# Output projection of the last two batches as seven block products instead of eight, with sums made by adding DMAs

## The chip, the cores and the metric

The kernel runs on one core of one Trainium2 chip. The metric is the device time of one execution in microseconds (us). A core has five engines that run side by side and wait for each other by semaphores: PE (TensorE, matrix products), DVE (VectorE), ACT (ScalarE), POOL (GpSimd) and SP (SyncE, which here only issues DMAs). PEld is PE's weight load, which overlaps its matmuls.

## The reference

Causal attention over 4 batches, 12 heads, 448 positions and head size 64 is followed by a gated feed-forward layer on all 1792 tokens:

```
scores = q @ k.T / sqrt(64), causal mask, softmax;  attn = softmax @ v
x   = attn, as [1792 tokens, 768]
g   = x @ w_gate        # 768 x 1536
val = x @ w_val         # 768 x 1536
h   = g * sigmoid(g) * val
out = h @ w_out         # 1536 x 768, float32
```

## The kernel before

**Layout and precision.** Everything is kept transposed: features lie on the 128 partitions and the 448 tokens of one batch along the free dimension. The 768 model features are 6 blocks of 128, the 1536 hidden features 12 blocks. Each float32 operand is split into a high and a low part (`hi` and `lo`, made by a copy and a subtraction, "a split" below), and one block product is three matmuls of 128x128 by 128x448: high by high, high by low, low by high. `halves` splits a block of activations, `weights` or `fetch_weights` loads a 128x768 tile of weights from a scratch copy in DRAM and splits it into `whl`.

**Batches.** Batches 0 and 1 go through `moe`: gate and value products (tile `M`), activation (`activate`, `finish_h`), output products (tile `MO`). Batches 2 (called A) and 3 (called B) are treated together at the end. `early` computes the first half of A's hidden blocks (`hA[0..5]`) and that half's share of A's output, for all six output blocks m, and stores that share in DRAM (`part`, `keepO`). `operands` and `pair(n)`, n = 0 to 5, compute the rest of A's hidden blocks (`hA[6..11]`) and all of B's (`hB[0..11]`) with a scheme of seven products in place of eight: sums of weight tiles and sums of activations are formed first (tiles `S1` to `S4`, `T1` to `T4`), and each product is accumulated into a sum for more than one result (tiles `Bb`, `Be`). `outputs` then does the output products that remain: for each m the second half of A (6 blocks) and all of B (12 blocks).

**Order.** Nothing of the order is fixed by the loops. Each piece of work is an `op` with the engines that may do it, costs, a due time, buffers and dependencies; `Planner.run` walks all operations once, giving each engine the ready operation that is due first, and the instructions are then issued engine by engine in the order found. Due times are sums of stage lengths (`LEN`), offsets and a table of several hundred numbers (`SHIFT`). Each engine works through its own list in order, so an instruction that waits holds up all behind it. All DMAs but a few stand on SP's list.

**Lines of the profile.** L1150 to L1152 are the three matmuls of gate, value and output products, L1466 to L1468 those of `pair`; L400 is a copy on ACT, L403 on DVE, L406 on POOL; L422 and L425 are a two-operand operation on DVE and on POOL; L1097 loads stored weights; L1230 stores a result; L1272 stores to a scratch tensor in DRAM; L1289 copies a half-done gate product out of PSUM; L1488 and L1492 belong to `pair`'s return of that half; L1606 forms a result of A.

The output products of A's first half are these:

```
for m in range(KD):
    prev, rM = project(A, m, range(HF), lambda x: at(4 * HF + 2 * m + x * 2 / HF), lambda f: A * NW + 2 * NF + 2 * m, hA,
                       lambda f: (hh(A, f), hl(A, f)), (A, "part", m), "M")
```

Of the kernel before, what the change touches and what calls it, by code (L numbers as in the profile page):

```python
# [1715 lines left out]
```

## Time and profile before

| | |
|---|---|
| median of 3 runs | 634.03 us (632.47 to 634.48) |
| profiled execution | 632.45 us, of which 630.7 us span from the first to the last instruction |
| PE busy | 623.1 us (99% of the span) |
| DVE busy | 517.0 us (82%) |
| ACT busy | 416.9 us (66%) |
| POOL busy | 251.3 us (40%) |
| granted TensorE clock | 1.00 in every slice |

Busy time is the time in which at least one instruction of the engine was in progress. Two matmuls that follow each other overlap in the records, so a busy PE need not be issuing at its best rate; the distance between the starts of two matmuls tells that.

### The profile page before, as it was taken

The page shows a single profiled execution, that of the slowest core. Times are in us where ns is not written, and L with a number is a line of the kernel's source. Part 1 is how long each engine was busy: PE and PEld are TensorE (multiplying, and loading weights), DVE is VectorE, ACT ScalarE, POOL GpSimd, SP SyncE. Part 2 cuts the span into 40 slices and gives each one's busy share as a digit, 9 for nine tenths or more (in the row PEclk, how much of TensorE's full clock was granted, in tenths as well). Part 3 has the DMA queues.
Part 4 walks back from the last instruction along what each step waited for, and adds up shares of the span by engine and source line. Part 5 has one row for each costly group of instructions (what it writes and reads, how often), then busy time and mean ns, then how long its engine had stood idle before and what let it go on. Part 6 is the DMA issues. An engine that isn't in the chain of part 4 may idle for free.

```text
span 630.7 us, 11116 instructions
## 1 busy us (share of the span) xinstructions
PE 623.1 (99%) x3590; PEld 561.2 (89%) x3590; DVE 517.0 (82%) x1168; ACT 416.9 (66%) x1001; POOL 251.3 (40%) x301
## 2 busy tenths in 40 slices
PE   8999999999999999999999999999999999999997
PEld 5557999999999999999999998889999999999997
DVE  5998999989998998988998889799988889975210
ACT  6998658958997678577687899775554454561110
POOL 3665543444356455435445453440034324440000
PEclk9999999999999999999999999999999999999999
DMA  8979597888996987576677877886444343236301
GB/s 284 333 245 335 139 384 276 281 318 293 307 362 167 320 267 246 149 249 220 177 224 252 271 239 201 251 283 230 136 121 130 129 131 102 86 109 190 105 18 70
DMA packets 72666, 136.07 MB, mean 216 GB/s; under 512 B 18080, under 2 KB 45472, under 8 KB 72608
## 3 DMA queue, kind: packets, MB, share of 16 engines
q1 hardware_dynamic: 72304, 135.04, 65.5%
q8 instruction: 28, 0.46, 0.3%
q10 hardware_dynamic: 304, 0.33, 0.2%
q14 instruction: 30, 0.25, 0.1%
HBM read 98.34 MB, written 37.00 MB: 215 GB/s over the span
## 4 chain that ended last, share of the span: by engine, by line
PE 83%; DVE 6%; DMA 5%; ACT 4%; issue 1%; POOL 0%; ACTq 0%; SPq 0%; DVEq 0%; POOLq 0%
PE M L1150 10%; PE M L1151 10%; PE M L1152 10%; PE MO L1150 9%; PE MO L1151 9%; PE MO L1152 9%; PE S L618 7%; PE O L1017 5%; DMA wr<-wr 3%; PE T L842 2%; PE O L1062 2%; PE Bb L1467 2%; PE Bb L1466 2%; PE Bb L1468 2%; PE Be L1468 1%
## 5 line engine op out<-in xcount | busy, mean ns | idle before, releaser
L1150 PE MATMUL M<-xh,whl 128*128 128x448 f32 x360 | 133.7, 371 | 0.9 <-ACT s L1289 0.7
L1152 PE MATMUL M<-xh,whl 128*128 128x448 f32 x360 | 130.4, 362 | 0.0
L1151 PE MATMUL M<-xl,whl 128*128 128x448 f32 x360 | 130.4, 362 | 0.0
L422 DVE TENSOR_TENSOR whl<-wraw,whl 128x768 fp32r<-128x768 f32 x86 | 83.9, 983 | 21.1 <-ACT whl L400 20.7
L681 ACT ACTIVATE p<-p,m 128x192 f32<-128x192 f32 (+3 forms) x180 | 91.1, 509 | 2.3 <-DVE m L669 2.0
L400 ACT ACTIVATE whl<-wraw 128x768 fp32r<-128x768 f32 x72 | 60.2, 840 | 34.1 <-PE MO L1152 19.8
L1150 PEld LDWEIGHTS M<-xh,whl 128*128 128x128 f32 x360 | 67.5, 188 | 7.8 <-ACT s L1289 2.8
L1152 PEld LDWEIGHTS M<-xh,whl 128*128 128x128 f32 x360 | 67.5, 187 | 4.7
L669 DVE CUSTOM_DVE_ANT_0 p<-S,masks 128x192 f32<-128x192 f32 (+3 forms) x180 | 68.3, 424 | 3.5 <-PE S L618 3.3
L1151 PEld LDWEIGHTS M<-xl,whl 128*128 128x128 f32 x360 | 67.6, 188 | 3.8
L1150 PE MATMUL MO<-h,whl 128*128 128x448 f32 x162 | 59.7, 369 | 0.0
L1151 PE MATMUL MO<-h,whl 128*128 128x448 f32 x162 | 58.7, 362 | 0.0
L1152 PE MATMUL MO<-h,whl 128*128 128x448 f32 x162 | 58.5, 361 | 0.0
L735 ACT ACTIVATE p<-p,rec 128x192 f32<-128x192 f32 (+3 forms) x128 | 53.9, 478 | 4.6 <-DVE rec L692 4.5
L1136 DVE SCALAR_TENSOR_TENSOR wraw<-wide,top 128x768 uint32<-128x768 uint32 x36 | 36.0, 1000 | 1.9 <-ACT top L400 1.8
L900 DVE STREAM_TRANSPOSE w<-p 128x256 f32<-128x256 f32 (+2 forms) x120 | 36.3, 354 | 0.6 <-ACT p L735 0.3
L618 PEld LDWEIGHTS S<-KS,QS 64*128 64x128 f32 (+1 forms) x432 | 29.6, 174 | 6.3 <-issue 4.1
L681 ACT ACTIVATION_READ_ACCUMULATOR p<-p,m 128x1 f32 (+1 forms) x180 | 34.1, 190 | 0.0
L425 POOL TENSOR_TENSOR whl<-wraw,whl 128x768 fp32r<-128x768 f32 x16 | 29.5, 1848 | 9.2 <-DVE whl L422 3.1
L1150 PE MATMUL MO<-last,whl 128*128 128x448 f32 x90 | 33.1, 368 | 0.0
L1151 PE MATMUL MO<-last,whl 128*128 128x448 f32 x90 | 32.6, 363 | 0.0
L1152 PE MATMUL MO<-last,whl 128*128 128x448 f32 x90 | 32.6, 362 | 0.0
(386 smaller groups left out, 1527.5 us busy)
## 6 DMA issues: line engine op xcount, KB each, us to landing
wide<-in_w_dram SPq DMA_DIRECT2D x36, 768.0 KB, 6.8
wraw<-wr SPq DMA_DIRECT2D x66, 384.0 KB, 4.1
wr<-wraw SPq DMA_DIRECT2D x36, 384.0 KB, 4.2
wr<-wr SPq DMA_DIRECT2D x24, 384.0 KB, 3.8
x<-dO SPq DMA_DIRECT2D x12, 608.0 KB, 6.0
vraw<-in_v_dram SPq DMA_DIRECT2D x24, 256.0 KB, 4.4
qraw<-in_q_dram SPq DMA_DIRECT2D x23, 224.0 KB, 5.0
kraw<-in_k_dram SPq DMA_DIRECT2D x23, 224.0 KB, 5.0
```

Of the source, the lines that this page charges most:

```text
L400: nc.scalar.activation(out(), in_(), AF.Copy, scale=scale)
L422: r["DVE"] = (cost("DVE", "two", n), lambda: nc.vector.tensor_tensor(out(), a(), b(), alu))
L618: nc.tensor.matmul(st[u + y][f"S{i}"][:r], Q[:, q0 : q0 + r], K[:, :q1_] if y else K[:, S - q1_ :], start=z == 0, stop=z == len(passes) - 1)
L669: nc.vector.tensor_tensor_reduce(p[:r], s[f"S{i}"][:r], mask[:r, maskX - q0 : maskX - q0 + q1_] if h % 2 else back[:r, P - min(q1_, P) : P ...
L681: nc.scalar.activation(p[:r], p[:r], AF.Exp, bias=peak(i)[:r], scale=-1.0, accum_out=sums[u % NR][:r, i : i + 1],)
L735: nc.scalar.activation(p[:r], p[:r], AF.Copy, scale=rec[u % NR][:r, i : i + 1])
L900: nc.vector.transpose(to, src)
L1017: nc.tensor.matmul(o, s["VS"][:, j, :m], p, start=x == 0, stop=x == len(todo) - 1)
L1136: nc.vector.scalar_tensor_tensor(w["raw"].bitcast(U32), z, 13, top, ALU.logical_shift_right, ALU.bitwise_or)
L1150: nc.tensor.matmul(out[:, :n], a[:, w], xhi, start=first, stop=False, skip_group_check=True)
L1151: nc.tensor.matmul(out[:, :n], a[:, w], xlo, start=False, stop=False, skip_group_check=True)
L1152: nc.tensor.matmul(out[:, :n], l[:, w], xhi, start=False, stop=bool(last), skip_group_check=True)
```

## The change

The output projection of A and B is one product of a 2 x 2 block matrix (output blocks 0 to 2 and 3 to 5; hidden blocks 0 to 5 and 6 to 11) with a 2 x 2 block matrix (hidden blocks; A and B). Before it is done as eight block products of 3 output blocks by 6 hidden blocks, 54 matmuls each. The change does it as seven:

- `early` keeps one of them (output blocks 0 to 2, A's first half) and drops the other; `keepO` shrinks from six tiles to three. All twelve hidden blocks of A are also stored in DRAM (`keepH`), twelve new DMAs of 224 KB on SP.
- `outputs` does six block products, one a phase (`phase0` to `phase5`, three products of 18 matmuls each). Phases 1 to 4 use sums of weight tiles, phases 1, 2, 3 and 5 sums of hidden blocks. Some hidden blocks are computed with the opposite sign, so that each sum is an addition.
- The sums of hidden blocks (`first_sum` to `fourth_sum`, six each) and one sum of weights in each of the three columns of phase 1 are made by a DMA that adds its source to its destination in SBUF (`gather`, on POOL's list). The other sums of weights (nine) are done by DVE or POOL. Each sum is then split.
- The planner runs three times: after each of the first two runs, the due time of each operation becomes its latest start that would not delay the end (`latest`), and the numbers of `SHIFT`, all new, are added in the last.
- The two steps that transpose attention's weights through DRAM read an odd head back into the tile it was written from, not into another; all tiles of the pool are laid out at the start (`place_all`).

```diff
-LEN = [57.293, 137.864, 266.214, 76.452, 83.944, 91.479]
+LEN = [57.293, 137.864, 266.214, 76.452, 83.944, 75.0]
...
+PASSES = 2
...
-    "": 0.77, "attention0": -24.87, "attention1": -21.61, "attention10": 3.28, "attention11": 4.59, "attention12": 0.29, "attention13": -0.26,
...
+    "": 0.25, "attention0": -39.18, "attention1": 0.84, "attention10": 1.77, "attention11": 7.53, "attention12": -0.13, "attention13": -0.06,
...
     def run(self, caps):
+        nd, extra = [o.nd for o in self.ops], [o.extra for o in self.ops]
+        order = self.once(caps)
+        for i in range(PASSES):
+            self.latest(order)
+            for o, n, x in zip(self.ops, nd, extra):
+                o.nd, o.extra, o.due = n, x, o.late + (o.shift if i == PASSES - 1 else 0.0)
...
+            order = self.once(caps)
+        return order
...
+    def gather(out, src, due, deps, use, kb, alloc=()):
+
+        return op({"POOL": (PDMA, lambda: nc.gpsimd.dma_start(out(), src(), accum_op=ALU.add))}, due, deps, alloc, use, extra=PLAT + kb / 160)
...
-        for m in range(KD):
+        for m in range(HK):
             prev, rM = project(A, m, range(HF), lambda x: at(4 * HF + 2 * m + x * 2 / HF), lambda f: A * NW + 2 * NF + 2 * m, hA,
                                lambda f: (hh(A, f), hl(A, f)), (A, "part", m), "M")
...
+        def first_sum(k):
+            res = [Res(f"xs{2 * k}"), Res(f"xs{2 * k + 1}")]
+            ld = op({"SP": (0.3, lambda: nc.sync.dma_start(xs[k], keepH[k])), "kb": 224}, at(HK) - AHEAD - 6, [kept["h", k]], res)
+            o, r_, t_ = hB[k]
+            d = (gather(lambda: xs[k], t_, at(HK) - AHEAD + 0.1 * k, [ld, o], res + r_, 224) if "T" in ACC else
...
+            a = op(copies("sbuf", T, to[0], lambda: xs[k], -1.0), at(HK) - AHEAD + 1 + 0.1 * k, [d], alloc[:1], res + (rs[:1] if not alloc else []))
+            l = op(minus(T, to[1], lambda: xs[k], lambda: raw(to[0]())), at(HK) - AHEAD + 2 + 0.1 * k, [a], alloc[1:],
...
+        def second_sum(k):
+            d1, split, res = sums_["x", k]
+            o, r_, t_ = hB[k + HF]
+            d = (gather(lambda: xs[k], t_, at(2 * HK) - AHEAD + 0.1 * k, split + [o], res + r_, 224) if "T" in ACC else
...
+            ops_[2, k], places[2, k] = halves(lambda: xs[k], to, at(2 * HK) - AHEAD + 1 + 0.1 * k, [d], res, [Res(f"xh{k}"), Res(f"xl{k}")]), to
...
+        def phase0(m):
+            src, ld, rw = fetch((0, m), W(m, 1), at(m) - 12 * WLEAD)
+            wo, rhl = divide((0, m), src, at(m), [ld], [rw])
...
+            last = product(0, m, ("c", m), "MMS"[m], rc, True, lambda k: (hA[k + HF], (lambda: hh("A2", k), lambda: hl("A2", k))), wo, rhl, [])
...
+            result(A, m, at(m + 1), [last, ld], [rc, rp], lambda: ps["c", m][:, :T], lambda: ps["back", m], scale=-0.5)
...
+        def phase1(m):
...
+                d = op({"SP": (0.3, lambda: nc.sync.dma_start(new(), scratch1[ga])), "kb": 384}, at(HK + m) - 16 * WLEAD, [stored[ga]], [rS])
+                d = gather(lambda: sums_[m], lambda: scratch1[gb], at(HK + m) - 12 * WLEAD, [d, stored[gb]], [rS], 384)
...
+            last = product(1, m, ("e", m), "STO"[m], re_, True, lambda k: (ops_[1, k], places[1, k]), wo, rhl, [])
...
+        def phase2(m):
+            src, ld, rw = fetch((3, m), W(m, 0), at(2 * HK + m) - 12 * WLEAD)
+            wo, rS = sums_["s", m]
+            d = op(binary(WC, lambda: sums_[m], lambda: sums_[m], src), at(2 * HK + m) - 8 * WLEAD, [ld, *wo], [], [rS, rw])
...
+            last = product(2, m, ("b", m), "XXM"[m], rb, True, lambda k: (ops_[2, k], places[2, k]), wo, rhl, [])
...
```

**Where POOL's list ends.** These are rows of POOL's list before, the last ones, near the end of `pair(5)` and at the start of `outputs` (`hraw`, `last`, `xh`, `xl`, `h` are blocks of B and their splits):

```order
L425 TENSOR_TENSOR hraw_7002<-hraw_7002,xs_73 128x448
L425 TENSOR_TENSOR S_5_7066<-wr_5_0_6924,top 128x384
L425 TENSOR_TENSOR S_5_7066<-wr_5_1_6956,top 128x384
L406 TENSOR_SCALAR S0hl_7091<-wr_5_1_6958 128x384
L425 TENSOR_TENSOR last_5282<-hraw_0_6669,last_5282 128x448
L406 TENSOR_SCALAR xh_79<-hraw_1_6900 128x448
L425 TENSOR_TENSOR xl_85<-hraw_1_6900,xh_79 128x448
```

The change puts the adding DMAs there; `xs_71` to `xs_76` hold the running sums for k = 0 to 5, `top` and `So` are sums of weights, `wr` the stored weights:

```order
L489 DMA top<-wr_203 128x768
L489 DMA xs_73<-hraw_0_6622 128x448
L489 DMA xs_71<-hraw_0_6271 128x448
L489 DMA xs_74<-hraw_6799 128x448
L489 DMA So_7158<-wr_205 128x768
L489 DMA xs_75<-hraw_6955 128x448
L489 DMA xs_76<-hraw_7160 128x448
L489 DMA xs_72<-hraw_0_6449 128x448
L489 DMA xs_75<-hraw_6955 128x448
L489 DMA xs_76<-hraw_7160 128x448
```

Arithmetic has left POOL's end, and 27 DMAs stand there, each with its own waits; of `xs_76`, the last pair's, the first sum and the second stand three places apart.

**The link on DVE.** DVE's list in the change, from the last pair's first block of B (`hB[5]`, first row) to the split of the first sum for k = 5 (last row; `T1hl` holds the splits of the first sums for k = 3 to 5, `hl` those of the output weights):

```order
L481 TENSOR_TENSOR hraw_7160<-hraw_7160,xs_76 128x448
L481 TENSOR_TENSOR So_6971<-So_6971,wo_0_7078 128x768
L481 TENSOR_TENSOR hl_1_7244<-top,hl_1_7244 128x768
L1240 SCALAR_TENSOR_TENSOR last_5435<-xs_72,last_5435 128x448
L481 TENSOR_TENSOR xl_85<-xs_73,xh_79 128x448
L1740 SCALAR_TENSOR_TENSOR osb_0_7274<-Nc_7113,back_7101 128x448
L481 TENSOR_TENSOR hl_2_7267<-So_7158,hl_2_7267 128x768
L1240 SCALAR_TENSOR_TENSOR T1hl_7151<-xs_75,T1hl_7140 128x448
L481 TENSOR_TENSOR top<-top,wo_1_7111 128x768
L481 TENSOR_TENSOR xl_83<-xs_71,xh_77 128x448
L481 TENSOR_TENSOR hl_1_7153<-wo_1_7054,hl_1_7153 128x768
L1240 SCALAR_TENSOR_TENSOR T1hl_7151<-xs_76,T1hl_7140 128x448
```

Before, the list ran from the same block to splits of weights that wait for nothing but their load:

```order
L1533 SCALAR_TENSOR_TENSOR xs_76<-tg_1_7246,xs_76 128x448
L422 TENSOR_TENSOR h_7271<-tmp('t21', 5)_7201,h_7228 128x448
L422 TENSOR_TENSOR hraw_7192<-hraw_7192,xs_76 128x448
L422 TENSOR_TENSOR whl_7258<-wraw_7121,whl_7258 128x768
L1606 SCALAR_TENSOR_TENSOR osb_0_7289<-MO_0_7156,back_7106 128x448
L422 TENSOR_TENSOR whl_7190<-wraw_7099,whl_7190 128x768
```

What moved: between the block of B and the split that PE needs there now stand ten other operations and, on POOL's list, an adding DMA; three rows ahead of the first one shown stands the operation that reads the last matmuls of `pair(5)`, and between them `h` and `hl_0`, the latter a split of 768 columns.

**Where PE comes to need them.** PE's list in the change, at the first matmul that uses the first sum for k = 5 (`Ne_7292<-T1hl_7140`, row 3182 of PE's list):

```order
L1725 MATMUL Nc_7331<-h_6499,hl_1_7153 128x448
L1726 MATMUL Nc_7331<-h_6554,hl_1_7153 128x448
L1727 MATMUL Nc_7331<-h_6499,hl_1_7153 128x448
L1725 MATMUL Ne_7292<-T1hl_7140,hl_2_7267 128x448
L1726 MATMUL Ne_7292<-T1hl_7151,hl_2_7267 128x448
```

and, 42 rows further on, at the first that uses the second sum for k = 5 (`xh_82`, row 3224):

```order
L1726 MATMUL Nb_7405<-xl_84,hl_1_7361 128x448
L1727 MATMUL Nb_7405<-xh_78,hl_1_7361 128x448
L1725 MATMUL Nb_7378<-xh_82,hl_0_7355 128x448
L1726 MATMUL Nb_7378<-xl_88,hl_0_7355 128x448
L1727 MATMUL Nb_7378<-xh_82,hl_0_7355 128x448
```

The last matmul of `pair(5)` is row 3109, so 72 matmuls stand between it and row 3182. In the list before, the rows behind `pair(5)` use splits made straight from blocks of A and B, none of them written by a DMA:

```order
L1466 MATMUL Be_1_7109<-xh_82,S4hl_7101 128x448
L1467 MATMUL Be_1_7109<-xl_88,S4hl_7101 128x448
L1468 MATMUL Be_1_7109<-xh_82,S4hl_7101 128x448
L1150 MATMUL MO_0_7234<-last_5282,whl_7131 128x448
L1151 MATMUL MO_0_7234<-last_5282,whl_7131 128x448
```

## Rows read from the trace of the kernel before

**Rows 1.** The page: the span, and busy time, share and instructions of each engine.

```profile
span 630.7 us, 11116 instructions
PE 623.1 (99%) x3590; PEld 561.2 (89%) x3590; DVE 517.0 (82%) x1168; ACT 416.9 (66%) x1001; POOL 251.3 (40%) x301
```

**Rows 2.** Busy time by stretch: window, length, engines, clock, DMA share, GB/s.

```profile
core 0: us, PE busy (x) PEld busy (x) DVE busy (x) ACT busy (x) POOL busy (x), PEclk, DMA share, GB/s
0.00:60.00 60.00, 57.17 (x423) 37.03 (x423) 49.34 (x162) 51.36 (x161) 30.46 (x51) 1.00 0.86 297
...
376.00:420.00 44.00, 43.03 (x232) 37.96 (x230) 38.22 (x93) 35.61 (x82) 19.60 (x24) 1.00 0.84 256
420.00:480.00 60.00, 60.00 (x311) 56.38 (x310) 54.11 (x88) 32.62 (x59) 13.95 (x13) 1.00 0.53 164
480.00:540.00 60.00, 59.90 (x300) 55.81 (x299) 49.90 (x71) 27.98 (x46) 22.73 (x21) 1.00 0.35 116
...
554.00:631.00 77.00, 73.05 (x366) 68.12 (x364) 26.36 (x35) 16.71 (x27) 7.00 (x7) 1.00 0.29 92
```

**Rows 3.** The page: the chain that ended last, by engine.

```profile
PE 83%; DVE 6%; DMA 5%; ACT 4%; issue 1%; POOL 0%; ACTq 0%; SPq 0%; DVEq 0%; POOLq 0%
```

**Rows 4.** Timeline of PE in `outputs`: start, length, line; the first and last matmuls.

```profile
554.28 0.36 PE L1150 MATMUL MO<-h,whl 128*128 128x448 f32 x1
554.48 0.36 PE L1151 MATMUL MO<-h,whl 128*128 128x448 f32 x1
554.68 0.36 PE L1152 MATMUL MO<-h,whl 128*128 128x448 f32 x1
...
626.68 0.36 PE L1152 MATMUL MO<-xh,whl 128*128 128x448 f32 x1
```

**Rows 5.** Waits of PE's weight loads for the half-done gate products in `early`.

```profile
PEld M L1150 <- ACT s L1289: 2.8, 5, 0.8
```

**Rows 6.** Timeline of DVE at the last attention heads of batch 3 and after.

```profile
444.29 1.27 DVE L422 TENSOR_TENSOR xs<-O,tmp 64x448 f32<-64x448 f32 x2
445.60 0.56 DVE L422 TENSOR_TENSOR S<-wr 128x384 f32<-128x384 f32 x1
446.08 0.55 DVE L422 TENSOR_TENSOR S<-wr,wr 128x384 f32<-128x384 f32 x1
...
454.99 0.62 DVE L422 TENSOR_TENSOR T2hl<-T,T2hl 128x448 fp32r<-128x448 f32 x1
```

**Rows 7.** Timeline of DVE where nothing kept it waiting, in `outputs`.

```profile
568.04 0.61 DVE L422 TENSOR_TENSOR hraw<-hraw,xs 128x448 f32<-128x448 f32 x1
568.58 0.95 DVE L422 TENSOR_TENSOR whl<-wraw,whl 128x768 fp32r<-128x768 f32 x1
569.48 0.62 DVE L1606 SCALAR_TENSOR_TENSOR osb<-MO,back 128x448 f32<-128x448 f32 x1
```

**Rows 8.** Groups of DVE, 480 to 631 us: count, busy and mean ns, idle before.

```profile
L422 DVE TENSOR_TENSOR whl<-wraw,whl 128x768 fp32r<-128x768 f32 x12 | 12.3, 1027 | 18.9 <-ACT whl L400 18.7
L422 DVE TENSOR_TENSOR S3hl<-S,S3hl 128x768 fp32r<-128x768 f32 x4 | 5.7, 1415 | 0.0
```

**Rows 9.** Groups of ACT, 480 to 631 us.

```profile
L400 ACT ACTIVATE last<-hraw 128x448 fp32r<-128x448 f32 x5 | 2.9, 576 | 1.1 <-PE Be L1468 1.0
```

**Rows 10.** DMA issues: engine, count, KB each, median us from issue to landing.

```profile
wide<-in_w_dram SPq DMA_DIRECT2D x36, 768.0 KB, 6.8
wraw<-wr SPq DMA_DIRECT2D x66, 384.0 KB, 4.1
...
out_dram<-osb SPq DMA_DIRECT2D x23, 224.0 KB, 2.1
...
last<-dO SPq DMA_DIRECT2D x1, 608.0 KB, 8.1
```

**Rows 11.** Timeline of the end: the last result's copy and its store.

```profile
627.13 0.54 ACT L400 ACTIVATE osb<-MO 128x448 f32<-128x448 f32 x1 [10.62 <-PE MO L1152]
627.71 0.35 ACTq L1230 DMA_DIRECT2D out_dram<-osb  x1
```

**Rows 12.** A group of the page: copies of weights on DVE alone.

```profile
L403 DVE TENSOR_SCALAR whl<-wraw 128x768 fp32r<-128x768 f32 x12 | 7.0, 583 | 11.1 <-PE MO L1152 10.8 <-PE M L1152 0.2
```

More of the change, by code (lines that the diff above doesn't have):

```diff
@@ L132, in __init__ @@
         self.tag, self.left, self.end = tag, 0, 0.0
+        self.users, self.owner, self.next = [], None, None
 class Op:
-    __slots__ = ("hop", "port", "kind", "soft", "kb", "alts", "due", "deps", "alloc", "uses", "extra", "idx", "nd", "outs", "start", "end", "eng", "fn")
+    __slots__ = ("hop", "port", "shift", "late", "kind", "soft", "kb", "alts", "due", "deps", "alloc", "uses", "extra", "idx", "nd", "outs", "start", "end", "eng", "fn")
     def __init__(self, alts, due, deps, alloc, uses, extra):
@@ L158, in op, with latest, once @@
         return o
-    def run(self, caps):
+    def latest(self, order):
+        end, after = max(o.end for o in order), None
+        for o in sorted(order, key=lambda o: o.start)[::-1]:
+            t = end
+            for d in o.outs:
+                lag = 0.0 if o in d.soft else o.extra + (LAT[o.eng] if d.eng != o.eng else (0.0 if o.eng == "PE" else 0.13))
+                t = min(t, d.late - lag)
+            for r in o.uses:
+                if r.next is not None:
+                    t = min(t, r.next.owner.late - o.extra - LAT[o.eng])
+            if o.eng == "PE":
+                if after is not None:
+                    t = min(t, after.late)
+                after = o
+            o.late = t - (o.end - o.start)
+    def run(self, caps):
+        nd, extra = [o.nd for o in self.ops], [o.extra for o in self.ops]
[4 more added lines that the diff above has]
+                o.nd, o.extra, o.due = n, x, o.late + (o.shift if i == PASSES - 1 else 0.0)
+                for r in o.uses:
+                    r.left, r.end, r.next = len(r.users), 0.0, None
+            order = self.once(caps)
+        return order
+    def once(self, caps):
         free = dict.fromkeys(("PE", "DVE", "ACT", "POOL", "SP"), 0.0)
@@ L265, in run @@
                 q = slots(r.tag)
-                q.remove(next(h for h in q if h is None or not h.left))
+                h = next(h for h in q if h is None or not h.left)
+                q.remove(h)
                 q.append(r)
+                if h is not None:
+                    h.next = r
             for r in o.uses:
@@ L1591, in outputs @@
[L1591 to L1599 removed]
+        at = lambda s: start[B_ + 2] + LEN[B_ + 2] * s / (6 * HK)
@@ new lines, in product, with mm @@
+        def product(z, m, key, tag, res, begin, operand, wo, rhl, deps):
+            prev = None
+            for k in range(KD):
+                a, l, ra, rl = operand(k)[0]
+                def mm(k=k):
+                    if begin and k == 0:
+                        ps[key] = bank(tag, f"N{key[0]}{m}")
+                    hi, lo = (f() for f in operand(k)[1])
+                    cols = slice(k * P, k * P + P)
+                    sh, sl = hls[z, m][:, 0, cols], hls[z, m][:, 1, cols]
+                    nc.tensor.matmul(ps[key][:, :T], sh, hi, start=begin and k == 0, stop=False, skip_group_check=True)
+                    nc.tensor.matmul(ps[key][:, :T], sh, lo, start=False, stop=False, skip_group_check=True)
+                    nc.tensor.matmul(ps[key][:, :T], sl, hi, start=False, stop=k == KD - 1, skip_group_check=True)
+                new = begin and k == 0
+                prev = op({"PE": (m3, mm)}, at(HK * z + m + k / KD), [prev, a, l, *wo] + (deps if k == 0 else []),
+                          [res] if new else [], [rhl, ra, rl] + ([] if new else [res]))
+            return prev
@@ new lines, in result, with new @@
+        def result(c, m, due, deps, res, src, other=None, final=False, scale=0.5):
+            ro = Res("osb")
+            def new():
+                ps[c, "s", m] = buf([P, T], F32, "osb", "osb", f"osb{c}_{m}")
+                return ps[c, "s", m]
+            if other:
+                e = op({"DVE": (two, lambda: nc.vector.scalar_tensor_tensor(new(), src(), scale, other(), ALU.mult, ALU.add))}, due - BOOST, deps, [ro], res)
+            else:
+                e = op(copies("psum", T, new, src, 0.5, engines="A" if final else "AD"), due - BOOST, deps, [ro], res)
+            put(c, m, due, e, ro, final)
+            return e
@@ new lines, in phase4 @@
+        @named
+        def phase4(m):
+            src, ld, rw = fetch((6, m), W(m, 1), at(4 * HK + m) - 12 * WLEAD)
+            wo, rS = sums_["s", m]
+            d = op(binary(WC, lambda: sums_[m], src, lambda: sums_[m]), at(4 * HK + m) - 8 * WLEAD, [ld, *wo], [], [rS, rw])
+            wo, rhl = divide((4, m), lambda: sums_[m], at(4 * HK + m), [d], [rS])
+            e, re_ = lower[m]
+            last = product(4, m, ("e", m), None, re_, False, lambda k: (ops_[4, k], places[4, k]), wo, rhl, [e])
+            _, _, ru, u2 = upper[m]
+            result(B_, m, at(4 * HK + m + 1), [last, u2], [re_, ru], lambda: ps["e", m][:, :T], lambda: ps["ou2", m])
@@ new lines, in phase5 @@
+        @named
+        def phase5(m):
+            src, ld, rw = fetch((7, m), W(m + HK, 1), at(5 * HK + m) - 12 * WLEAD)
+            wo, rhl = divide((5, m), src, at(5 * HK + m), [ld], [rw])
+            u3, rb, _, _ = upper[m]
+            last = product(5, m, ("b", m), None, rb, False, lambda k: (ops_[5, k], places[5, k]), wo, rhl, [u3])
+            result(A, m + HK, at(5 * HK + m + 1), [last], [rb], lambda: ps["b", m][:, :T], final=m == HK - 1)
+        for k in range(KD):
+            first_sum(k)
@@ new lines, in outputs @@
+        for k in range(KD):
+            second_sum(k)
+        for m in range(HK):
+            phase0(m)
+        for k in range(KD):
+            third_sum(k)
+        for m in range(HK):
+            phase1(m)
+        for k in (0, 1, 2, 3, 4, 5):
+            plain(k)
+        for m in range(HK):
+            phase2(m)
+        for k in range(KD):
+            fourth_sum(k)
+        for m in range(HK):
+            phase3(m)
+        for m in range(HK):
+            phase4(m)
+        for m in range(HK):
+            phase5(m)
```

247 lines of the change are left out of this document (167 added, 80 removed), and 101 rows, old and new, of the table SHIFT.

## The prediction

> **What bounds the kernel now.** I read the page's first part first: PE is busy 623.1 of 630.7 us, the next engine, DVE, 517.0 [rows 1]. Busy need not mean working at its best rate, so I looked next at the stretches and the timeline. From 60 us on PE is busy in all but 1.0 us of 376 to 420 and 0.1 us of 480 to 540, and the clock is 1.00 [rows 2]; in `outputs` matmuls start every 0.20 us, and 363 of them, from 554.28 to 626.68, take 72.4 us for 362 steps: 0.200 us each, with nothing lost [rows 4]. The chain of waits says the same, PE holds 83% of it [rows 3]. What PE doesn't use lies in three places: 2.8 us in the first 60 [rows 2], 1.0 around the half-done gate products, which wait for a copy on ACT (2.8 us of waits of weight loads in the whole run) [rows 2, 5], and 3.7 us at the end, from the last matmul's end (626.68 + 0.36 = 627.04) over a copy and a store to 630.7 [rows 1, 4, 11]. So a matmul removed is worth 0.20 us, as long as the other engines can feed PE that much sooner.
>
> The reader should also see how full DVE is: 88% ahead of `outputs` (517.0 - 26.4 = 490.6 of 554 us), 34% in it (26.4 of 77) [rows 1, 2]. POOL and ACT have room everywhere.
>
> **The change, part by part.**
>
> *Matmuls.* PE's list has 3474 rows before and 3420 in the change; the 54 are one block product of `early`, output blocks 3 to 5 by A's first six hidden blocks. 54 x 0.200 = 10.8 us less. From the first output matmul to the end there are 363 rows before and 363 in the change, so `outputs` stays 72.6 us long and begins 10.8 us sooner, at about 543.5: the whole gain has to be made ahead of it.
>
> *Can DVE feed that?* Ahead of the first output split DVE has 1114 rows before and 1090 in the change: `early` loses three splits of weights, and other work went to ACT and POOL. At the mean of 517.0 / 1151 = 0.45 us a row that is some 11 us less; 480 of 543 us is 88% again. The planner's new due times move nearly every row, and what that gives or costs no row tells; before, 3.9 us of idle PE lie ahead of 554 us (2.8 + 1.0 + 0.1) [rows 2], so I put it between 2 us gained and 3 lost, and take 0. The place where the 10.8 us bite is the joint between batch 3's attention and `pair(0)`. Before, from the sum of the last two heads on DVE at 444.29 to the end of the third `T2hl` split at 454.99 + 0.62 = 455.61 it took 11.3 us [rows 6], and PE had 66 matmuls, 13.2 us, from the last attention matmul to the first that uses it. In the change 45 matmuls stand there, 9.0 us, and 11 rows of DVE: two of 64 partitions (1.3 us [rows 6]), six of 448 columns, two of 384, one of 768. Where nothing waits, 448 columns take 0.54 us from start to start and 768 take 0.90 [rows 7]; 384 take 0.48 (445.60 to 446.08 [rows 6]). That is 1.3 + 3.2 + 1.0 + 0.9 = 6.4 us; with some 0.9 us from PE's end over ACT to DVE (0.36 for the matmul, 0.54 for the copy [rows 4, 11]) it is 7.3 of 9.0. It fits with 1.7 us to spare, as before (13.2 less 11.3 + 0.9: 1.0). If POOL's reads make DVE's rows as slow as the slowest group (1.4 us for 768 columns, half as much again [rows 8]), the 6.4 become 9.6 and PE waits 1.5 us. I take 0.6, nearer the undisturbed rows, since most rows in [rows 6, 7] are undisturbed.
>
> *Work added in `outputs`.* From its first split to its end DVE's list has 81 rows in the change, 28 of 768 columns and 53 of 448: 28 x 0.90 + 53 x 0.54 = 53.8 us of 72.6, against 26.4 of 77 before [rows 2, 7]. ACT's 62 rows at 0.58 to 0.85 us (0.576 for 448 columns [rows 9]) are some 40 us. Both fit, DVE less comfortably. Twelve stores of `keepH` on SP (224 KB) replace three of `keepO`; they stand on a list that waits for DVE most of its time already, and the stored blocks are wanted 60 us and more later, the last ones 20.
>
> *Adding DMAs.* No row shows one. Bounds: from below a plain store of 224 KB, 2.1 us from issue to landing; from above the 608 KB that took 8.1, since an adding DMA reads its source, reads its destination and writes it, 672 KB in all [rows 10]. By bytes it is nearest to the rows of 384 KB (4.1) and 768 KB (6.8): 4.1 + 2.7 x 288 / 384 = 6.1 us. I take that.
>
> Are 6.1 us hidden? From the last matmul of `pair(5)` to the first use of the first sum for k = 5 stand 72 matmuls, and 42 more to the first use of the second sum: 114 x 0.200 + 0.2 = 23.0 us. The path through it: 0.36 to the matmul's end, on DVE the block's factor, `h`, a split of weights and the product (0.54 + 0.54 + 0.90 + 0.54 = 2.5 [rows 7]), a first DMA, a copy on ACT (0.58 [rows 9]) and a split on DVE (0.54), a second DMA, copy and split again: 0.4 + 2.5 + 1.1 + 1.1 = 5.1, and eight hand-overs at 0.2 (one took 0.1, 627.04 to 627.13 [rows 4, 11]), 6.7. That leaves 16.3 us for two DMAs, 8.1 each. DVE's ten other rows beside the first DMA take 5 x 0.90 + 5 x 0.54 = 7.2 us and its nine beside the second 5.6, so they don't decide. At 6.1 us the path has 4 us to spare, at 8.1 none. The third and fourth sums have 20 us and more.
>
> What could make the DMAs slower is their own number. In about 78 us (the loads begin some 6 ahead of `outputs`) the change moves 21 tiles of weights (8.3 MB), 23 blocks loaded or stored (5.3 MB) and 27 adding DMAs, 6.7 MB counted once and 13.4 with the destination read too: 260 or 345 GB/s. Before, 116 GB/s filled 0.35 of the DMA engines, so 331 fill them [rows 2]. The truth lies between 0.78 and 1.04 full. For that, and for DVE at 74%, I take 1.2 us of waits in `outputs` (bounds 0 and 5).
>
> *What the Trainium skill says of this.* "DMA: Bandwidth & Descriptors", "Anatomy of one DMA", fits a DMA issued from GpSimd with 2.0 us and bytes / 436e3: an estimate of 2.5 us for 224 KB by that page; with it the 1.2 us would be 0 and the result 623.8. Speaking against the change, "SBUF — State Buffer", "SBUF: two separate sides", says that GpSimd can't write the descriptors of its DMAs while DVE runs a copy in its two-port mode. DVE's copy of 768 columns takes 583 ns against 900 for two operands [rows 7, 12], so there is a faster mode; but the last such copy on DVE's list in the change is row 837 of 1172, far ahead of the first adding DMA. Were every DVE row to hold up a DMA once, 6.1 would become 7.0, still under 8.1; no run here shows it.
>
> *The end.* The last product is copied by ACT and stored as before: 3.7 us.
>
> **Sum.** 632.45 (the profiled execution) - 10.8 + 0.6 + 1.2 = 623.4. The median of the runs shown is 1.6 above that execution, so the forecast for the median is **625.0 us**, 9.0 or 1.4% less.
>
> **Rivals.**
> - *The adding DMAs land late* (after 8.1 us each): for, 27 of them on one list in order, each waiting for its own sum, and DMA engines up to full; against, the rows of up to 768 KB land in 6.8 at the median. At 10 us the path is 6.7 + 20 - 23.0 = 3.7 us too long: 625.0 + 3.7 = 628.7.
> - *DVE sets the pace* in `outputs` and at the joint: for, 74% and 71% of the time at undisturbed rates, and rows of 1.4 us for 768 columns [rows 8]; at that rate `outputs` needs 28 x 1.4 + 53 x 0.62 = 72 us of DVE, as much as PE. Against, POOL does no arithmetic there. Some 4 us: 629.
> - *Slower than before*: the same list of POOL, but DMA engines full. Each DMA then queues behind loads of 384 KB, and the waiting one holds up all behind it. The path loses more than the 9.0 gained from 6.7 + 2g - 23.0 > 9.0, g = 12.7 us; at 14 us (three loads of 4.1 ahead [rows 10] and its own 2.1) 625.0 + 11.7 = 636.7. For: the upper count of 345 GB/s. Against: no group of rows has a median above 8.1.
> - *No change*: DVE, at 88%, keeps its pace ahead of `outputs` and PE waits the 10.8 us away: 634. Against: its list lost rows there too.
>
> **Numbers.** The forecast 0.56 (621 to 628), late DMAs 0.17, DVE 0.11, no change 0.06, slower 0.10. A measurement of this kernel tells 0.3%, 1.9 us. Faster is 0.56 + 0.17 + 0.11 = 0.84, same 0.06, slower 0.10. The range holds the first three and leaves the rest out: 620.8 (2 us gained by the new order, none lost in `outputs` and the joint, 625.0 - 1.8 - 2, rounded down a little) to 631.5 (late DMAs, 628.7, and almost 3 us lost to the new order).
>
> **What would show it.** Right: PE with 54 fewer matmuls and 0.20 us steps in `outputs`, first output matmul near 543, adding DMAs landing in 4 to 8 us, DVE busy some 54 to 60 us in the last 77. Wrong: gaps in PE ahead of the uses of `T1hl` or `xh` with an adding DMA as the last wait; DVE without idle time there; or idle PE at 430 to 450. If adding DMAs take over 12 us the sign is wrong.

## The result, and where the time came from

The changed kernel takes 627.38 us (median of 4 runs, 626.35 to 628.27), the kernel before 633.25 on the same chip (632.17 to 634.48): a ratio of 0.9906, 95% interval 0.988 to 0.9933. That is 5.9 us faster where 9.0 were forecast, inside the stated range. The profiled execution took 626.35, and its span is 6.1 us shorter than that of [rows 1].

The page of the changed kernel: the span, the engines' busy time, and (last line) the chain that ended last by engine.

```profile
span 624.6 us, 11141 instructions
PE 613.6 (98%) x3536; PEld 551.6 (88%) x3536; DVE 527.3 (84%) x1189; ACT 440.1 (70%) x1041; POOL 257.2 (41%) x324
...
PE 75%; DMA 10%; DVE 7%; ACT 5%; issue 2%; SPq 0%; POOL 0%; ACTq 0%; DVEq 0%; POOLq 0%
```

PE has the 54 instructions fewer (3590 to 3536), and its share of the chain falls from 83% [rows 3] to 75%, with DMA at 10% where it was 5%. The stretches say where PE now waits:

```profile
core 0: us, PE busy (x) PEld busy (x) DVE busy (x) ACT busy (x) POOL busy (x), PEclk, DMA share, GB/s
0.00:60.00 60.00, 57.54 (x413) 39.03 (x415) 46.64 (x160) 49.29 (x144) 30.53 (x55) 1.00 0.80 266
...
376.00:420.00 44.00, 43.87 (x249) 40.26 (x248) 39.04 (x90) 36.84 (x87) 21.61 (x29) 1.00 0.88 268
420.00:480.00 60.00, 58.03 (x291) 53.10 (x290) 55.17 (x94) 36.22 (x64) 12.35 (x12) 1.00 0.49 168
480.00:540.00 60.00, 60.00 (x301) 56.23 (x301) 50.98 (x80) 27.46 (x47) 18.27 (x18) 1.00 0.53 156
540.00:600.00 60.00, 57.44 (x278) 51.12 (x278) 44.64 (x66) 30.28 (x50) 15.58 (x18) 1.00 0.93 240
```

The last of these stretches in the kernel before:

```profile
540.00:600.00 60.00, 60.00 (x302) 56.24 (x301) 35.38 (x49) 21.70 (x35) 12.22 (x12) 1.00 0.39 125
```

Beside [rows 2] this is a gain of 0.8 us of busy PE at 376 to 420, a loss of 2.0 at 420 to 480, and one of 2.6 at 540 to 600, where PE was busy throughout before and the DMA engines' share was 0.39. Busy time hides part of it, since a matmul that starts late counts as busy while it drains. So I add up, over the timeline of PE, what each step from one 448-column matmul to the next takes beyond 0.200 us:

| stretch | before | after | what PE waits for, after |
|---|---|---|---|
| to 380 | 5.8 | 5.6 | |
| 380 to 420 | 2.6 | 0.5 | half-done gate products |
| 420 to 480 | 0.0 | 3.1 | accumulators at the joint, 445 and 449 (1.9); a half-done gate product at 424 (0.7); a sum of weights at 479 (0.5) |
| 480 to 540 | 0.4 | 0.0 | |
| 540 to 600 | 0.0 | 4.6 | 1.8 at the end of `pair(5)`; in `outputs` 1.1 at 560 to 580 and 1.7 at 580 to 600 |
| sum | 8.7 | 13.8 | |

That closes the sum: -10.8 for 54 matmuls, +5.0 of losses, and 0.4 us less idle time in the first 60 us against 0.1 more at the end, which is -6.1, the measured difference of the spans. (The row up to 380 depends by some tenths on how the short matmuls of attention are counted; its change hardly does.)

PE's timeline at three places: the joint, the end of `pair(5)` with the first output matmul, and the last one.

```profile
444.21 0.37 PE L1198 MATMUL MO<-h,whl 128*128 128x448 f32 x1
445.21 0.47 PE L1518 MATMUL Bb<-T2hl,S2hl 128*128 128x448 f32 x1 [0.63 <-ACT part L459]
...
448.73 0.37 PE L1520 MATMUL Bb<-T2hl,S2hl 128*128 128x448 f32 x1
449.79 0.47 PE L1518 MATMUL Bb<-xh,S3hl 128*128 128x448 f32 x1 [0.70 <-ACT u L1550]
...
542.03 0.37 PE L1520 MATMUL Bb<-xh,S3hl 128*128 128x448 f32 x1
543.95 0.47 PE L1518 MATMUL Bb<-xh,S3hl 128*128 128x448 f32 x1 [1.56 <-ACT u L1550]
...
545.27 0.36 PE L1725 MATMUL Nc<-h,hl 128*128 128x448 f32 x1
...
620.47 0.36 PE L1727 MATMUL Nb<-xh,hl 128*128 128x448 f32 x1
```

`outputs` now lasts 75.2 us from its first matmul to its last, 72.4 before [rows 4], and begins 9.0 us sooner, not 10.8. At 445 and 449 PE waits for an accumulator to be emptied (by ACT, and by DVE and ACT after each other), not for an operand. At 543 it is the same kind of wait, but ACT itself was held up. This is ACT's list there, and under it the piece of the chain that released it:

```profile
540.08 0.85 ACT L459 ACTIVATE S4hl<-S 128x768 fp32r<-128x768 f32 x1 [0.64 <-PE Bb L1520]
542.62 0.84 ACT L459 ACTIVATE hl<-wo 128x768 fp32r<-128x768 f32 x1 [1.70 <-DMA wo<-wr]
543.37 0.96 ACT L1550 ACTIVATE u<-Bb 128x448 f32<-128x448 f32 x2
```
```profile
536.54 6.00 DMA wo<-wr
```

The copy of the first output weights stands ahead of `u<-Bb` on ACT's list and waits for their load, which took 6.00 us; PE pays for it. The 2.8 us in `outputs` have two sources. At 560 to 580 the longest wait goes back to an adding DMA, one that sums weights (`So`, 9.3 us, the longest of the 27); at 580 to 600 VectorE waits for loads of weights:

```profile
563.62 0.84 ACT L459 ACTIVATE hl<-So 128x768 fp32r<-128x768 f32 x1 [2.37 <-DMA So<-wr]
```
```profile
584.43 0.96 DVE L481 TENSOR_TENSOR wo<-wo,wo 128x768 f32<-128x768 f32 x1 [0.72 <-DMA wo<-wr]
591.60 0.96 DVE L481 TENSOR_TENSOR So<-wo,So 128x768 f32<-128x768 f32 x1 [0.93 <-DMA wo<-wr]
```

The chain that ended last also runs over two adding DMAs before it comes to these loads:

```profile
557.95 8.25 DMA xs<-hraw
567.46 5.72 DMA xs<-hraw
```

What loaded the DMA engines there is in the queues' view of 530 to 600 (MB, share of the engines' time; then one group of issues with its median to landing):

```profile
q1 hardware_dynamic: 4830, 11.07, 47.4%
q0 software_dynamic: 3087, 5.42, 44.9%
...
wo<-wr SPq DMA_DIRECT2D x18, 384.0 KB, 4.6
```

q0 holds the adding DMAs. They move a third of the bytes and take nearly half of the engines' time. From issue to landing they take (least, median, most of the 27, by the line that issues them):

```profile
DMA to landing us min/median/max: 3.1/5.7/9.3
```

### The profile page after: what moved, and what is told of

Read it like the earlier page. It is cut to its first block, busy times and chain, and to the rows that moved or that the text cites. A ratio compares the mean times of both kernels' runs of the same rounds, so it can differ in the third digit from the quotient of the medians.

```text
span 624.6 us, 11141 instructions
## 1 busy us (share of the span) xinstructions
PE 613.6 (98%) x3536; PEld 551.6 (88%) x3536; DVE 527.3 (84%) x1189; ACT 440.1 (70%) x1041; POOL 257.2 (41%) x324
## 4 chain that ended last, share of the span: by engine, by line
PE 75%; DMA 10%; DVE 7%; ACT 5%; issue 2%; SPq 0%; POOL 0%; ACTq 0%; DVEq 0%; POOLq 0%
PE M L1196 9%; PE M L1197 9%; PE M L1198 9%; PE S L673 6%; PE MO L1196 5%; PE MO L1198 5%; PE MO L1197 5%; PE O L1065 4%; PE Bb L1518 3%; PE Bb L1520 3%; PE Bb L1519 3%; PE O L1110 2%; DMA xs<-hraw 2%; DMA wo<-wr 2%; PE T L897 2%
## 5 line engine op out<-in xcount | busy, mean ns | idle before, releaser
L736 ACT ACTIVATE p<-p,m 128x448 f32<-128x448 f32 (+3 forms) x180 | 91.2, 508 | 4.4 <-DVE m L724 4.1
L481 DVE TENSOR_TENSOR whl<-wraw,whl 128x768 fp32r<-128x768 f32 x78 | 77.8, 1004 | 5.2 <-ACT whl L459 4.5
L459 ACT ACTIVATE whl<-wraw 128x768 fp32r<-128x768 f32 x67 | 56.3, 841 | 18.8 <-PE M L1198 12.9
L790 ACT ACTIVATE p<-p,rec 128x448 f32<-128x448 f32 (+3 forms) x123 | 56.1, 503 | 1.6 <-DVE rec L747 1.5
L1196 PE MATMUL MO<-h,whl 128*128 128x448 f32 x102 | 37.8, 371 | 0.0
L1198 PE MATMUL MO<-h,whl 128*128 128x448 f32 x102 | 37.0, 362 | 0.0
L1197 PE MATMUL MO<-h,whl 128*128 128x448 f32 x102 | 36.9, 361 | 0.0
L794 POOL TENSOR_SCALAR p<-p,rec 128x320 f32<-128x320 f32 (+3 forms) x49 | 24.3, 504 | 23.9 <-DVE p L798 9.6
L673 PE MATMUL S<-KS,QS 64*128 64x448 f32 (+3 forms) x432 | 32.2, 295 | 0.0
L1065 PE MATMUL O<-ph,VS 128*128 128x448 f32 (+3 forms) x144 | 31.0, 303 | 0.0
L465 POOL TENSOR_SCALAR top<-wide 128x768 f16<-128x768 bf16 x18 | 19.5, 1084 | 26.0 <-DVE wraw L1182 8.1
```

The source lines that it names most:

```text
L459: nc.scalar.activation(out(), in_(), AF.Copy, scale=scale)
L481: r["DVE"] = (cost("DVE", "two", n), lambda: nc.vector.tensor_tensor(out(), a(), b(), alu))
L673: nc.tensor.matmul(st[u + y][f"S{i}"][:r], Q[:, q0 : q0 + r], K[:, :q1_] if y else K[:, S - q1_ :], start=z == 0, stop=z == len(passes) - 1)
L736: nc.scalar.activation(p[:r], p[:r], AF.Exp, bias=peak(i)[:r], scale=-1.0, accum_out=sums[u % NR][:r, i : i + 1],)
L790: nc.scalar.activation(p[:r], p[:r], AF.Copy, scale=rec[u % NR][:r, i : i + 1])
L1065: nc.tensor.matmul(o, s["VS"][:, j, :m], p, start=x == 0, stop=x == len(todo) - 1)
```

## Experiments

Two theories on the 4.6 us at 540 to 600: the DMA engines are so full that *other* transfers come late ("load"), or the path over two adding DMAs is too long ("path"). A third question is what the 54 matmuls are worth, and a fourth whether the sums have to be DMAs at all. Ratios are to the kernel before, run beside it on the same chip; the runs come from several chips.

**e1: adding DMAs of 8 columns.** Nothing else moves.

```
-nc.gpsimd.dma_start(out(), src(), accum_op=ALU.add)
+nc.gpsimd.dma_start(out()[:, :8], src()[:, :8], accum_op=ALU.add)
```

> The changed kernel, its instructions and their order as they are, but each of the 27 adding DMAs moves 8 columns where it moved 448 or 768; the rest of each sum is left out. The profile of the changed kernel loses 1.7 us of TensorE time at 542 (ScalarE's copy of a weight block waits for a load of 6.0 us) and 2.8 us in the output projection. Theory 'DMA engines too full': the adding DMAs' bytes make loads and sums late, so nearly all of that comes back and the time falls by 2.5 to 4.5 us, to 623 to 625; loads of 384 KB in the output projection land in about 4 us. Rival 'the order does it' (where loads stand on SP's list, VectorE's and ScalarE's lists, accumulator banks): the bytes hardly matter, 626 to 628.

622.86 us, ratio 0.9826 (0.9802 to 0.985): 4.5 us less than the changed kernel by the medians. The stretch, the loads of output weights (KB each, median to landing) and the adding DMAs' landing times in e1:

```profile
540.00:600.00 60.00, 59.09 (x296) 54.95 (x295) 47.28 (x71) 32.45 (x54) 16.46 (x19) 1.00 0.60 170
```
```profile
wo<-wr SPq DMA_DIRECT2D x18, 384.0 KB, 3.8
```
```profile
DMA to landing us min/median/max: 2.0/2.8/6.1
```

PE has 1.7 us more busy time there; of the 4.6 us of losses 1.2 stay (one wait near 590), and that at 543 is gone. So the adding DMAs' bytes cost most of what was lost, but both theories can say so: the sums land in 2.8 us, and the loads in 3.8 for 4.6.

**e2: more load, no step added to the path.** Beside each adding DMA a copy of 224 KB within main memory on SP's list, for which nothing waits. The copies stand between the loads of weights on that list.

```
 nc.gpsimd.dma_start(out(), src(), accum_op=ALU.add)
+nc.sync.dma_start(spare.pop(), scratch1[0][:, :T])
```

> The changed kernel, with one more DMA of 224 KB from one place of main memory to another, on SP's list, beside each of the 27 adding DMAs; nothing waits for it. That adds 6 MB read and 6 MB written to the last 105 us. Theory 'DMA engines too full': loads of weights and sums come later still, PE waits 4 to 12 us more, 631 to 640. Rival 'the order does it': there is room for it, less than 2 us more, 627 to 629.5.

637.73 us, ratio 1.0067 (1.0042 to 1.0091): 10.4 us more.

```profile
540.00:600.00 60.00, 52.62 (x237) 45.82 (x236) 36.63 (x55) 26.43 (x45) 14.78 (x17) 0.94 0.99 278
```

At a share of 0.99 the load theory's range holds; there is no room left. But late loads and late sums still come together: the sums land in 6.7 us at the median, and PE waits for their splits too.

**e6 and e9: short sums under load.** The adding DMAs of 8 columns, and behind each on POOL's list a plain copy within main memory, of 224 KB in e6 (shown below) and of 360 KB in e9.

```
-nc.gpsimd.dma_start(out(), src(), accum_op=ALU.add)
+nc.gpsimd.dma_start(out()[:, :8], src()[:, :8], accum_op=ALU.add)
+nc.gpsimd.dma_start(spare.pop(), scratch1[0][:, :T])
```

> The changed kernel with adding DMAs of 8 columns, as in e1, and behind each of them on POOL's list a plain DMA of 224 KB from one place of main memory to another, for which nothing waits: the load stays near what the changed kernel has, the sums' own DMAs are short. Most of each sum is left out. Theory 'the load on the DMA engines makes other transfers late': most of what e1 gained is lost again, 625.5 to 628.5. Rival 'the path over two adding DMAs is too long': what e1 gained stays, 622 to 624.

> As e6 (adding DMAs of 8 columns, most of each sum left out, and a plain DMA behind each on POOL's list), with plain DMAs of 360 KB where e6 had 224 KB: per byte the adding DMAs of the changed kernel took about 1.6 to 1.9 times the DMA engines' time of plain ones, so this brings the load in the output projection back to that of the changed kernel (0.93 between 540 and 600, where e6 had 0.82 and e1 0.60). Theory 'the path over two adding DMAs is too long': still 622.5 to 624.5. Rival 'the load makes the other transfers late': 626 to 629.

e6 took 623.42 us, ratio 0.9853 (0.9829 to 0.9877); e9 took 627.44, ratio 0.9901 (0.9877 to 0.9925). The stretch in e6, then in e9:

```profile
540.00:600.00 60.00, 58.99 (x293) 54.41 (x292) 47.06 (x71) 32.64 (x54) 27.62 (x40) 1.00 0.82 246
```
```profile
540.00:600.00 60.00, 56.62 (x279) 51.72 (x279) 44.69 (x68) 31.07 (x51) 26.67 (x38) 1.00 0.89 283
```

e6 kept nearly all that e1 gained and so spoke for the path; e9, with the load brought near that of the changed kernel, speaks against it. The lists are the same, and the sums' own DMAs land in 3.8 and 4.4 us at the median where the changed kernel has 5.7, so e9's path is the shorter; yet e9's time is the changed kernel's. The wait at 543 is back in e9, and so is its cause:

```profile
543.63 0.84 ACT L459 ACTIVATE hl<-wo 128x768 fp32r<-128x768 f32 x1 [1.90 <-DMA wo<-wr]
```

In e6 the same copy did not wait, though its loads of output weights land in 4.6 us at the median, as in the changed kernel: the median of 18 loads tells nothing here, the one load ahead of `u<-Bb` does (6.00 us, and 5.11 in e9 by its chain).

By share of 540 to 600 the five kernels of one order stand in a row: 0.60 gives 622.9, 0.82 gives 623.4, 0.89 gives 627.4, 0.93 (the changed kernel) 627.4, 0.99 gives 637.7. Against the kernel before beside each of them that is -10.6, -9.5, -5.2, -5.9 and +4.3 us, and e9's six runs alone lie between 623.3 and 628.9, so the steps between neighbours are not to be read finely. That load alone brings the loss back is shown. How the changed kernel's 4.6 us divide between late loads and late sums is not: the sums slow with the load as well (2.8, 3.8, 4.4 and 5.7 us), and a late sum can push back a list and with it the next load. The changed kernel loses 1.1 us at 560 to 580, where its longest wait goes back to an adding DMA, and e9 loses nothing there; I take that as an estimate of the sums' own part.

**e10: a long path with little load.** Each small adding DMA is made twice, on the same columns, so that the second waits for the first to land (the edit against e1).

```
+for _ in range(2):
     nc.gpsimd.dma_start(out()[:, :8], src()[:, :8], accum_op=ALU.add)
```

> As e1 (adding DMAs of 8 columns, most of each sum left out), with each adding DMA made twice, the second after the first has landed: nearly no load, but 4 to 6 us from the first issue to the second landing, about what the changed kernel's adding DMAs of 224 KB take (5.7). Theory 'the path is too long': what e1 gained is lost, 626 to 629. Rival 'the load does it': 622.5 to 624.5 as e1.

656.29 us, ratio 1.0373 (1.035 to 1.0397): neither. What POOL waited for, and then who waited for the DMAs (us in total, times), from that line's view:

```profile
  DMA xs<-hraw: 28.1, 12
  DMA xs<-kh: 14.1, 7
  DMA hraw<-hraw: 12.2, 6
```
```profile
  ACT xh L459: 24.6, 9
```

The second of each pair waits on POOL's own list and holds up every DMA behind it, for 54 us in all in these three groups. The run doubled the path and blocked the list at once, so it can't price the path; it shows that a POOL list which waits for landings is far dearer than either theory.

**e3 and e5: the kernel before with fewer matmuls.** e3 left out more than its text says: its condition reached the products of `outputs` by A's second half as well, 90 matmuls and not 45. e5 leaves out the 45 alone; its edit, where the cut line only closes the accumulation:

```
+if c == A and m >= HK and fs[0] == 0 and x:
+    return
...
```

> The kernel before, in its own order, where the output blocks 3 to 5 of the early part get one of six products by A's first half; the other 45 matmuls are left out, and so is their part of the result. Theory 'a matmul ahead of the output projection is worth its 0.200 us': 9.0 us less with up to 2 us of it lost to work that now stands closer, so 624 to 626.5. Rival 'VectorE, 88% busy ahead of the output projection, keeps the pace': most of the 9.0 are waited away, 629 to 633.

> The kernel before, in its own order, with 45 matmuls fewer, all of them in the early part: its output blocks 3 to 5 get one of six products by A's first half, and their part of the result is wrong. (The run of the kernel before with fewer matmuls, e3, had reached the output projection's products by A's second half as well, and left out 90.) Theory 'the joint loses its cover': the 9.0 us come off, and 3 to 4.8 us of them are waited away between 420 and 480, where the changed kernel waits too, so 627 to 629.5. Rival 'a matmul is worth its 0.200 us there and the joint's waits belong to the changed kernel's order': 624 to 625.5, TensorE idle under 1 us between 420 and 480.

e3: 623.85 us, ratio 0.9846 (0.9825 to 0.9866), 9.6 us less for 18.0 us of matmuls. Its profile has the same two waits at the joint as that of e5 below (2.80 and 1.26 us), so most of its gain is that of the 45 matmuls in `outputs`. e5: 631.64, ratio 0.9982 (0.9965 to 0.9998): 1.3 us less for 9.0, above the range of either theory. PE in e5 at the joint, and the stretch after it:

```profile
445.23 0.37 PE L1152 MATMUL MO<-h,whl 128*128 128x448 f32 x1
448.42 0.48 PE L1468 MATMUL Be<-last,S1hl 128*128 128x448 f32 x1 [2.83 <-ACT S1hl L400]
448.74 0.37 PE L1469 MATMUL Be<-last,S1hl 128*128 128x448 f32 x1
450.36 0.74 PE L1470 MATMUL Be<-last,S1hl 128*128 128x448 f32 x1 [1.25 <-DVE S1hl L422]
450.90 0.57 PE L1468 MATMUL Be<-last,S1hl 128*128 128x448 f32 x1
451.27 0.57 PE L1469 MATMUL Be<-last,S1hl 128*128 128x448 f32 x1
```
```profile
448.00:457.00 9.00, 7.32 (x21) 5.99 (x22) 9.00 (x16) 6.33 (x12) 0.00 (x0) 0.62 0.45 129
```

DVE has no idle time at 448 to 457 and PE waits for `pair(0)`'s first weight sum, 2.83 and 1.25 us. Over that stretch its clock is granted at 0.62, matmuls step by 0.37 us from 450.9 to 456.6, and the joint costs 7.5 us in place of nothing. (This profiled execution took 633.93 us, the longest of the twelve, 2.3 above their median; a typical one loses less in all.) In the old order DVE does set the pace there, and the matmuls that were taken out had covered it. But e5 keeps all 1168 instructions of VectorE, with the three splits of weights that the change drops from `early`: it tests the matmuls alone, not the change's way of dropping them.

**e4: the changed kernel with its 54 early matmuls made twice**.

```
 mm3(ps[key], i, f % KD, T, hi, lo, x == 0, x == len(fs) - 1)
+if c == A:
+    mm3(ps[key], i, f % KD, T, hi, lo, x == 0, x == len(fs) - 1)
```

> The changed kernel, in its own order, where the early part makes each of its 54 matmuls of output blocks 0 to 2 twice (the first pass is overwritten or added once more, so three blocks of one batch are not the reference's). Theory 'each is worth 0.200 us, and the waits at the joint stay or shrink by up to 1.7 us': 9.1 to 10.8 us more, 636.5 to 638.2. Rival 'another engine keeps the pace there': under 5 us more, 628 to 632.

638.52 us, ratio 1.0078 (1.005 to 1.0106): 11.1 us more for 10.8 us of matmuls. That is just above the first theory's range. In the changed order each added matmul is paid in full, and more cover does not shrink the joint's waits (0.63 and 0.70 us before the same two matmuls, as without it).

**e7 and e8: no adding DMA for the sums** (e7), or for the three weight sums alone (e8); the rest on VectorE and POOL, and the planner finds the order anew.

```
-ACC = 'STU'
+ACC = ''
```

(e8: `'S'`.)

> The changed kernel with all its sums of hidden blocks and of weights made by VectorE and POOL, none by DMA; the planner finds the order anew with the same table, and VectorE gets 21 more instructions, POOL 13 fewer. Theory 'DMA engines too full': their load falls, 21 x 0.54 = 11 us more on VectorE fit into its idle 25% of the output projection, 623 to 626.5. Rival 'VectorE sets the pace there': it is over 85% busy from 420 on, and the time rises by 3 to 8 us, 630 to 635.

> The changed kernel with its 24 sums of hidden blocks made by VectorE and POOL, and the three sums of weights still by adding DMAs; order found anew with the same table. Theory 'DMA engines too full': 623 to 626.5, within 1 us of the kernel with no adding DMA. Rival 'VectorE sets the pace': 630 to 635.

639.76 us, ratio 1.0109 (1.0092 to 1.0126), and 639.78, ratio 1.0108 (1.0091 to 1.0125): above the range of either theory. In e7 VectorE is nearly full:

```profile
540.00:600.00 60.00, 53.30 (x253) 48.14 (x252) 56.54 (x85) 30.28 (x51) 13.28 (x11) 0.97 0.56 187
```
```profile
596.79 0.37 PE L1727 MATMUL Nb<-h,hl 128*128 128x448 f32 x1
604.47 0.74 PE L1725 MATMUL Nb<-h,hl 128*128 128x448 f32 x1 [7.31 <-ACT h L459]
```

That looks like VectorE's pace, but the order changed too, which e11 and e12 take away.

**e11 and e12: the same order, 18 of the 24 hidden sums as additions** where both operands lie on chip: on POOL in e11, in the place where the DMA was issued, on VectorE in e12.

```
+if src().space != bass.MemoryType.DRAM:
+    nc.gpsimd.tensor_tensor(out(), out(), src(), ALU.add)
+else:
     nc.gpsimd.dma_start(out(), src(), accum_op=ALU.add)
```

(e12: `nc.vector` in the second line.)

> The changed kernel in its own order, with 18 of its 24 hidden sums (those whose two operands both lie on chip) made by an addition on POOL in the place where the adding DMA was issued; the six sums with a block from main memory and the three of weights stay adding DMAs. 18 x 224 KB leave the DMA engines, and POOL gets 18 x some 1.2 us (448 columns of two operands took 1.16 us on it) in about 70 us. Theory 'the adding DMAs' load is what the changed kernel loses in the output projection': the stalls at 542 and near 590 shrink as in e1, 622.5 to 625. Rival 'POOL's additions slow VectorE and hold up POOL's list': 627 to 632.

> As e11, with the 18 additions on VectorE in place of POOL, each at the place in VectorE's list where the program issued it; the other lists are those of e11. In e7 and e8 VectorE was busy 56.5 and 55.5 of the 60 us from 540 and the time rose to 639.8, but the planner had also found another order. Theory 'VectorE has no room for them': 18 x 0.54 = 9.7 us more on a list that already has 44.6 to 50 of 60 us, waits of 3 us and more with TensorE at a lower clock behind them, 628 to 640. Rival 'it was the order found anew': 622.5 to 626, as e11.

e11: 622.96 us, ratio 0.9847 (0.9825 to 0.9869). e12: 625.03 us, ratio 0.9886 (0.9867 to 0.9905). The stretch and POOL's additions in e11, then the stretch in e12:

```profile
540.00:600.00 60.00, 58.09 (x288) 53.45 (x287) 50.12 (x69) 31.56 (x53) 21.16 (x19) 1.00 0.63 188
```
```profile
L491 POOL TENSOR_TENSOR xs<-xs,hraw x12: 1147/1162/1467, 521.9 to 569.2; 128x448 f32<-128x448 f32 x12
```
```profile
540.00:600.00 60.00, 57.86 (x286) 52.89 (x285) 52.48 (x81) 30.83 (x52) 3.51 (x5) 1.00 0.64 191
```

An addition on POOL takes 1.16 us where the DMA took 5.7, the DMA share falls to 0.63, and the loss at 543 from 1.8 to 0.9 us (1.3 in e12). It does not vanish: the share is a mean over 60 us, and the first of the four weight loads issued together there still took 4.74 us in e11 and 5.18 in e12, by their chains. e11 beats both kernels: its interval ends below that of the changed one. e12 is 2.1 us behind it and still ahead of the kernel before: VectorE had room for 18 additions, where e7 gives it 21 more, so most of what e7 and e8 lost came with the order found anew and not from the additions as such. Which move of that order does it is open.

## Why the prediction was partly right

- **Matmuls, -10.8: right as counted.** The 54 are gone, and e4 gives their price in the changed order (11.1 for 10.8 added). But the reason given, that a matmul removed is worth 0.20 us wherever the engines can feed PE, hid how narrow that is: e5 got 1.3 of 9.0 us in the old order. The rival "no change" (VectorE keeps its pace ahead of `outputs`) is what e5 shows; in the changed kernel it does not hold. Whether that is due to the new order or to the splits of weights that the change drops was not tried.
- **New due times, 0 between 2 gained and 3 lost: right as a bound.** 2.1 us came back at 380 to 420 around the half-done gate products, 0.7 of which one of them costs later, at 424. Their weight loads now wait 1.6 us where it was 2.8 [rows 5]:

```profile
PEld M L1196 <- ACT s L1340: 1.6, 3, 0.8
```

- **The joint, +0.6: too small.** It cost 1.9 us at 445 and 449, in the place where the prediction had named idle PE as a sign against it. All of 420 to 480 lost 3.1, and 4.1 to 4.7 in the profiles of e1, e6 and e9, which lose 1.8 to 2.2 at the wait near 479. The step counted VectorE's rows against PE's matmuls and left out that consecutive products of one accumulator pass through VectorE and ACT.
- **Adding DMAs, 6.1 us: right**, 5.7 at the median. But the path worked out for k = 5 left a transfer out: the first sum adds to a stored block of A, and its load into `xs_76` can't start before DVE's product `hraw`, which reads that tile. SP issued the load at 559.00, it took 7.4 us, and POOL's list waited for it:

```profile
566.92 1.75 POOL L489 DMA_DIRECT2D xs<-hraw  x2 [8.12 <-DMA xs<-kh]
570.70 0.62 DVE L1240 SCALAR_TENSOR_TENSOR T1hl<-xs,T1hl 128x448 fp32r<-128x448 f32 x1 [0.96 <-ACT T1hl L459]
571.69 0.36 PE L1727 MATMUL Ne<-T1hl,hl 128*128 128x448 f32 x1
```

The adding DMA behind it then landed in about 3.1 us and the split was done at 571.32, just as PE came to use it (0.06 us lost there). That nothing more was lost on this path is luck: the 4 us to spare went to a load for which the sum has no term, and an adding DMA shorter than the forecast made up for it. The fit of the Trainium skill, "DMA: Bandwidth & Descriptors", "Anatomy of one DMA" (2.0 us and bytes / 436e3, an estimate of 2.5 us for 224 KB by that page) is under every one of the 27: the least took 3.1. Its fixed part agrees with e1, where 4 KB landed in 2.0 at the least.
- **Waits in `outputs`, +1.2: the step that failed.** The range of the load held (0.78 to 1.04 full; 0.79 measured from 545 to 624, and 0.93 at 540 to 600), and the bounds of 0 to 5 held the truth, 4.6. But the value was taken near the low end because only the sums' own path was costed. The larger part fell on other transfers, loads of weights that stand on ACT's and VectorE's lists ahead of what PE needs: 1.8 us at 543, before the first output matmul, and 1.7 at 580 to 600, of which e1 still loses 1.2 with almost no bytes in its adding DMAs. The estimate of the load was right in part by luck: 545 to 624 moved 201 GB/s, fewer than the lower count of 260, and the engines' share still came inside because the adding DMAs took longer per byte (last section).
- **VectorE in `outputs`, 53.8 us: right.** 53.0 busy from 545 to 624, and it did not set the pace (e12). **The end, 3.7 us: right**, 3.8.

The forecast for the profiled run was 623.4 and it took 626.35. The misses are +3.4 at 540 to 600 (4.6 for 1.2), +2.5 at 420 to 480 (3.1 for 0.6, 1.9 of it at the joint), and -2.1 at 380 to 420, -0.4 at 480 to 540, -0.1 up to 380, -0.3 in idle time at the start and the end: 3.0, of the 2.95 that are off.

## What to carry to other kernels

A matmul taken out is worth its step only where its cover isn't needed: look for the engine that feeds PE and is busiest at the next change of stage (e5, 1.3 us of 9.0). When a change adds DMAs, don't only ask whether they themselves land in time, but which load on an in-order list will land later: here the DMA share could go from 0.60 to 0.82 for about 1 us, and to 0.89 for about 5. A sum whose operands both lie on chip was better left to an idle engine than to an adding DMA, in the place where the DMA stood (e11, 623.0 us for 627.4).
